# Moving the output weights' mean row to GpSimd, and moving sums, turns, squares and products in a Fourier and SoLU kernel

## The chip, the cores and the metric

The kernel runs on one core of one Trainium2 chip. The metric is the device time of one execution in microseconds. Five engines have queues of their own, each worked off in order: TensorE (PE in the profile, with its weight loads as PEld), VectorE (DVE), ScalarE (ACT), GpSimd (POOL) and SyncE (SP, which here only issues DMAs). POOL issues DMAs too. They wait for each other through semaphores.

## What is computed

The input x has 8 sequences of 3136 tokens with 256 features. Its two-dimensional Fourier transform over tokens and features is taken, and the real part goes through one expert:

```python
X = np.fft.fft(np.fft.fft(x, axis=1), axis=2).real     # (8, 3136, 256) -> (25088, 256)
h = X @ w_in                                            # 1024 hidden features
sm = softmax(h)
solu = h * sm
ln = (solu - solu.mean(-1)) / sqrt(solu.var(-1) + 1e-6) * g_ln
out = ln @ w_out                                        # (25088, 256)
```

All arithmetic is in 32-bit floats; the weights arrive as 64-bit floats and are narrowed on the chip.

## The kernel before, in words

**The transform.** 3136 is 49 x 64. The sequences go in four pairs (`pairs`). For each pair `load` fetches the rows and their mirror rows, `add_mirror` adds the two, `fold` or `fold_part` (L149, L150, L174) adds and subtracts the features k and 256 - k, `transform1` (L214) does the 49-point part on TensorE, `keep` writes the result to DRAM and `turn` (L230) reads it back with the other axis on the partitions. `transform2` (L242) does the 64-point part for one `k1`; `take2` (L248) copies its result to SBUF as `q`. The feature transform is multiplied into w_in once, at the start: `product_in` (L665) makes the even half of `Wi` (h = 0), its odd half (h = 1) and the row `w_mid` (h = 2, spread over all partitions), and `keep_in` (L669) copies each from PSUM.

**Units.** A unit is one `k1` of one pair: 128 rows, 25 units per pair, 100 in all. Except for k1 = 0 a unit has two signs: the hidden row is the even part plus or minus the odd part. `up` (L277) multiplies `q` with one half of `Wi` into a PSUM tile of two banks (`h0` or `h1`, one buffer each). `even` (L283) adds `r` times `w_mid` to the even part on DVE, where `r` is one row of `q` laid over the partitions, by a small DMA on SP (`spread`, L253) or, for units 2 and 3, by TensorE (`column`, L268 and L270). `join` (L291) makes h for a sign and its maximum, `expo` (L299) is exp on ACT, `product` (L306) multiplies h with it on DVE, `square` (L313) sums squares on ACT, `stats` (L326, L328) and `power` (L339, L368) make the scale per row. `join(s)` reads `ev`, or the sign 0 row, and the PSUM tile `h1`, so `up` of the next unit's odd half waits for it.

**Down.** The hidden rows are needed with the hidden features on the partitions. For units 0 to 3 `turn_whole` does that on TensorE: transposes (L394) of a sign go to two of the four banks `result(1..4)`, and copies bring them to `uT`, for sign 0 on ACT at once (L399), for sign 1 through the list `t.wait` on DVE (L868) or, in step 4, on ACT (L873). From unit 4 on `turn_both` (L377) transposes blocks of 32 x 32 on DVE, and `move_blocks` (L413) sends the blocks to their places, 16 DMAs on SP for two units. The product with w_out for a unit of two signs takes seven block products instead of eight (`Down`, L451): it needs four sums of parts of the rows (`sums`, L444, on POOL, the last three units' on DVE) and four sums of parts of the weights (`weight_sums`, L425, once, on POOL). `finish` scales and adds the blocks P5 (L508) and X (L510) on DVE and the rows are stored (L536 on POOL, the other half by SP). Units with one sign use `down` (L519). The layer norm's mean is taken out of w_out: `centre` sums the rows of `Wo` on TensorE (L698), scales the sum on ACT (L699), and subtracts it from `Wo` in one DVE instruction (L700).

**The order of the work** is written out by hand. Until the first pair's last first transform there is the weights' part: pieces of raw words are split into exponent and mantissa (`exponent`, `confine`, `narrow`; L571, L593 to L595, L607 to L615). Then comes the opening loop over steps 0 to 4 (`whole` = 4): step i turns unit i - 1, joins and finishes unit i, and begins unit i + 1 (`begin`: up, even, up, and the second transform of unit i + 3). Then the main loop: step i does up, even, join, expo, product, square and turn of unit i, the seven products of unit i - 5 (`lag`) and the sums of unit i - 4. The other pairs' mirror sums (POOL), folds (DVE), first transforms (PE) and loads are threaded into fixed steps; the folds of pair 1 run in steps 4 to 19. `behind(i, t)` makes an instruction wait for the last `product` of unit t; the helper gives as its reason "two operands at a time from SBUF".

Of the kernel before, what the change touches and what calls it, by code (L numbers as in the profile page):

```python
# [34 lines left out]
WHOLE = 4  # L35

# [7 lines left out]
def kernel(  # L44
# [187 lines left out]
    def transform2(pr, k1):  # L232

        i, k = divmod(k1, KG)
        g = pr.g[i]
        table = T[0][:, :, k, :] if i == 0 else T[1][:, :, k1 - KG, :]
        ps = result(0)[:, 0 : KD * P]
        for h in range(KD):  # L240
            o = ps[:, h * P : (h + 1) * P].rearrange("p (b k) -> p b k", b=2)
            nc.tensor.matmul(o, g[:, k, h * P : (h + 1) * P], table,  # L242
                             start=(h == 0), stop=True, skip_group_check=True)
        return ps
# [27 lines left out]
    def up(t, c):  # L272

        ps = ps_h.tile([P, FF], FP32, tag=f"h{c}", name=f"ps_h{c}")
        for half in range(2):
            fs = slice(half * HW, (half + 1) * HW)
            nc.tensor.matmul(ps[:, fs], t.q[:, c * P : (c + 1) * P], Wi[:, c, fs], start=True, stop=True)  # L277
        return ps

    def even(t, ps):  # L280

        t.ev = fpool.tile([P, FF], FP32, tag="ev", name="ev", bufs=1)
        nc.vector.scalar_tensor_tensor(out=t.ev, in0=w_mid, scalar=t.r, in1=ps,  # L283
                                       op0=ALU.mult, op1=ALU.add)
# [99 lines left out]
    def turn_whole(t):  # L384

        uT = t.batch.uT[:, t.w].rearrange("p c i (n s) -> p c (i n) s", s=2)
        n = KF // 2
        t.wait = []
        for s in t.signs:
            for half in range(2):  # L390
                ps = result(2 * s + half + 1).rearrange("p (c k) -> p c k", c=n)
                for c in range(n):
                    f = half * n + c
                    nc.tensor.matmul(ps[:, c, :], t.u[s][:, f * P : (f + 1) * P], ident, is_transpose=True,  # L394
                                     start=(c == 0), stop=(c == n - 1), skip_group_check=True)
                if s:
                    t.wait.append((uT[:, half * n : (half + 1) * n, :, s], ps))
                else:
                    nc.scalar.copy(uT[:, half * n : (half + 1) * n, :, s], ps)  # L399
# [21 lines left out]
    def weight_sums():  # L421

        B11, B12, B21, B22 = [Wo[:, k : k + KF // 2, f : f + P] for k in (0, KF // 2) for f in (0, P)]
        for j, (a, b) in enumerate(((B12, B11), (B22, Ws[:, 0]), (B22, B12), (B21, Ws[:, 1]))):
            nc.gpsimd.tensor_tensor(out=Ws[:, j], in0=a, in1=b, op=ALU.subtract)  # L425
# [27 lines left out]
    class Down:  # L453
# [52 lines left out]
        def finish(self):  # L506
            o = self.t.ot[0][:, P:]
            nc.vector.scalar_tensor_tensor(out=o, in0=self.P5, scalar=self.rs[0], in1=o, op0=ALU.mult, op1=ALU.add)  # L508
            o = self.t.ot[1].rearrange("p (i d) -> p i d", i=2)
            nc.vector.scalar_tensor_tensor(out=o, in0=self.X.unsqueeze(1).to_broadcast([P, 2, P]),  # L510
                                           scalar=self.rs[1], in1=o, op0=ALU.mult, op1=ALU.add)
# [71 lines left out]
    def confine(unit, here=False):  # L583

        if unit is None:
            return
        if here:
            bits(unit, unit, -896.0, ALU.add, 0.0, ALU.max)
            bits(unit, unit, 255.0, ALU.min, 2.0 ** 23, ALU.mult)
            return  # L590

        u = unit.bitcast(FP32)
        nc.scalar.activation(out=u, in_=unit, func=ACT.Relu, bias=limits[:, 0:1])  # L593
        nc.scalar.activation(out=u, in_=u, func=ACT.Relu, bias=limits[:, 1:2], scale=-1.0)
        nc.scalar.activation(out=unit, in_=u, func=ACT.Identity, bias=limits[:, 2:3], scale=-(2.0 ** 23))  # L595
# [22 lines left out]
    class Weights:  # L618
# [40 lines left out]
        def product_in(self, h):  # L659
            ps = ps_h.tile([P, FF], FP32, tag=f"h{h % 2}", name="wps")  # L660
            for half in range(2):
                fs = slice(half * HW, (half + 1) * HW)
                for c in range(KD):
                    lhsT = self.m[:, c, :] if h == KD else self.Q[:, c, h * P : (h + 1) * P]
                    nc.tensor.matmul(ps[:, fs], lhsT, self.w_in[c][:, fs], start=(c == 0), stop=(c == KD - 1))  # L665
            return ps
# [27 lines left out]
        def centre(self):  # L694

            cs = result(0)[:, 0:D]
            for c in range(KF):
                nc.tensor.matmul(cs, ones, Wo[:, c, :], start=(c == 0), stop=(c == KF - 1))  # L698
            nc.scalar.mul(out=wbar, in_=cs, mul=1.0 / FF)  # L699
            nc.vector.tensor_tensor(out=Wo, in0=Wo, in1=wbar.unsqueeze(1).to_broadcast([P, KF, D]), op=ALU.subtract)  # L700
# [41 lines left out]
    with tc.manual_schedule():  # L742
# [30 lines left out]
        for c in range(NC):  # L773
# [10 lines left out]
            if c == NC - 1:  # L784
                for i in range(3):
                    weights.exponent_out(i)
            if c + 6 < NC:
# [8 lines left out]
            for s in range(CH // 2):  # L796
                transform1(first, c * CH // 2 + s)
            if c == 3:
                weights.keep_in(0, weights.product_in(0))

        turn(first, 0, nc.sync, 0, 2)
        turn(first, 0, nc.gpsimd, 2, KG)

        middle = weights.product_in(KD)
        confine(weights.units[0], True)
        for i in range(1, 3):
            confine(weights.units[i])
        weights.keep_in(KD, middle)
        weights.narrow_out(0)
        weights.exponent_out(3)  # L810
        confine(weights.units[-1])
        odd = weights.product_in(1)
# [4 lines left out]
        for t in units[:2]:  # L817
            take2(t, transform2(pairs[0], t.k1))
            spread(t)
            if t is units[0]:  # L820
                weights.keep_in(1, odd)
# [6 lines left out]
        def second_transform(i):  # L828
            if i < len(units):
                t = units[i]  # L830
                take2(t, transform2(pairs[t.p], t.k1))
                if i not in (2, 3):
# [26 lines left out]
        for i in range(whole + 1):  # L859
            cur = units[i]  # L860
            prv = units[i - 1] if i else None
            if prv:
                turn_whole(prv)
            for s in cur.signs:
                join(cur, s)
            if prv and i < whole:
# [4 lines left out]
            if prv and i == whole:  # L871
                for o, ps in prv.wait:
                    nc.scalar.copy(o, ps)  # L873
            if i == 0:
                begin(1)
            if i == whole:
# [5 lines left out]
            if i == 1:  # L882
                weights.centre()
                weight_sums()
            if i < whole:

                if i:
                    begin(i + 1)
                if 1 in cur.signs:
                    square(cur, 1)  # L890
                stats(cur)
                power(cur)
            else:
                for s in cur.signs:
                    square(cur, s)
                other_pairs(i, ahead, "mirror", cur)
                turn_both(cur)
# [4 lines left out]
            for work in ("mirror", "fold", "load") if i < whole else ("load",):  # L902
                other_pairs(i, ahead, work)
# [5 lines left out]


        fresh = True
        for i in range(whole + 1, len(units) + lag + 1):
# [18 lines left out]
            if i == len(units):  # L931
                for s in prv.signs:
                    square(prv, s)
            if prv:
# [14 lines left out]
            elif old:  # L949
                for s, ps in plain:  # L950
                    scale(old, s, ps)
            if cur:
# [6 lines left out]
            if seven:  # L959
                new.p3()  # L960
                new.p7()
                new.finish()
            if cur:
                other_pairs(i, ahead, "mirror")
            if by_seven(i + 1 - lag):
# [8 lines left out]
            if cur:  # L974
# [8 lines left out]
                turn_both(cur)  # L983
# [92 lines left out]
```

## Time and profile before

| what | us |
|---|---|
| median of 3 runs (lowest, highest) | 1135.96 (1133.18, 1139.01) |
| the profiled execution, its own time | 1132.91 |
| its span | 1130.9 |
| PE busy | 1092.3 (97%) |
| DVE busy | 987.4 (87%) |
| ACT busy | 800.5 (71%) |
| POOL busy | 796.3 (70%) |

The profile tells of one execution. The chain of work that ended last follows the program back from its end, at each step to what released it; the groups give each line's instructions, their count, busy time and mean; the waits say who idled for whom; the timeline lists instructions by start and duration; the windows give each engine's busy time in a stretch. A start is counted from the start of the span. POOL's own durations are rough; the spacing of its instructions tells more.

### The profile page before, as it was taken

Reading aid. Unit: us, or ns where it says so; the run is one execution under the profiler, and the core shown is the slowest. Engines: PE = TensorE matmul, PEld = TensorE weight load, DVE = VectorE, ACT = ScalarE, POOL = GpSimd, SP = SyncE. Lnnn points to the kernel's source line nnn. Section 1 sums busy time; section 2 is a strip of 40 time slices with the busy share of each in tenths; the row PEclk is TensorE's granted clock in tenths of the full one; section 3 lists DMA queues with packets and bytes.
Section 4 is the critical chain, followed back from the end, with each engine's and each line's share of the span. In section 5 each row is a group of like instructions: output and inputs, shape, how many; then the busy total and the mean of one; then the engine's idle time right before and its main releaser. Section 6 shows DMA issues by size and latency. Waiting matters only on the chain.

```text
span 1130.9 us, 21944 instructions
## 1 busy us (share of the span) xinstructions
PE 1092.3 (97%) x7030; PEld 872.2 (77%) x7030; DVE 987.4 (87%) x1442; ACT 800.5 (71%) x1945; POOL 796.3 (70%) x698
## 2 busy tenths in 40 slices
PE   2898999999999999999999999999999999999998
PEld 1556787887887787878877787878877788778888
DVE  7889989898889998898988998898888899898983
ACT  4667777777767777777767777777776777777761
POOL 3036888875795988865878788876686576766673
PEclk9999999999999999999999999999999999999999
DMA  9672798766998879876969798876788685965665
GB/s 246 207 196 57 169 189 205 174 150 147 165 207 159 188 174 186 192 152 144 169 149 186 170 191 187 197 178 148 152 160 156 132 164 116 161 142 112 140 135 119
DMA packets 459601, 185.77 MB, mean 164 GB/s; under 512 B 426870, under 2 KB 441470, under 8 KB 459488
## 3 DMA queue, kind: packets, MB, share of 16 engines
q1 hardware_dynamic: 445728, 146.22, 63.0%
q0 software_dynamic: 13760, 38.16, 13.1%
q8 instruction: 57, 0.93, 0.3%
q14 instruction: 56, 0.46, 0.1%
HBM read 44.78 MB, written 38.80 MB: 74 GB/s over the span
## 4 chain that ended last, share of the span: by engine, by line
PE 90%; DVE 4%; issue 2%; ACT 2%; DMA 2%; SPq 0%; POOL 0%; POOLq 0%; DVEq 0%; ACTq 0%
PE ps_m L451 52%; PE ps_h L277 28%; PE ps_m L214 5%; PE ps_m L242 4%; DMA raw_in<-in_moe_w_in_dram 1%; DVE h L291 1%; DVE u L306 1%; PE ps_m L519 1%; ACT h L313 1%; DVE ev L283 0%; DVE y L150 0%; PE wps L665 0%; DVE Wo L615 0%; DVE y L149 0%; ACT u L299 0%
## 5 line engine op out<-in xcount | busy, mean ns | idle before, releaser
L277 PE MATMUL ps_h<-Wi,q 128*128 128x512 f32 x800 | 362.4, 594 | 5.9 <-DVE nmax L291 5.1
L444 POOL TENSOR_TENSOR S<-uT 128x512 f32<-128x512 f32 x186 | 238.0, 1279 | 108.3 <-DVE u L306 34.5
L451 PE MATMUL ps_m<-Ws,S 128*128 128x128 f32 x2304 | 296.4, 275 | 0.0
L451 PEld LDWEIGHTS ps_m<-Ws,S 128*128 128x128 f32 x2304 | 279.8, 192 | 3.6 <-issue 0.4
L313 ACT ACTIVATE h<-u,usum 128x1024 f32<-128x1024 f32 x196 | 225.3, 1150 | 79.5 <-DVE u L306 79.0
L277 PEld LDWEIGHTS ps_h<-Wi,q 128*128 128x128 f32 x800 | 143.8, 190 | 152.0 <-issue 139.4
L306 DVE SCALAR_TENSOR_TENSOR u<-h,u 128x1024 f32<-128x1024 f32 x196 | 234.7, 1234 | 9.4 <-ACT u L299 9.4
L299 ACT ACTIVATE u<-h,nmax 128x1024 f32<-128x1024 f32 x196 | 223.8, 1143 | 6.0 <-DVE nmax L291 4.7
L377 DVE STREAM_TRANSPOSE v<-u 128x2048 f32<-128x2048 f32 x88 | 203.4, 2311 | 3.1
L451 PE MATMUL ps_m<-Wo,uT 128*128 128x128 f32 x1536 | 203.7, 276 | 0.0
L451 PEld LDWEIGHTS ps_m<-Wo,uT 128*128 128x128 f32 x1536 | 187.9, 192 | 1.0 <-issue 1.0
L291 DVE CUSTOM_DVE_ANT_0 h<-ev,ps_h 128x1024 f32<-128x1024 f32 x100 | 122.2, 1222 | 17.0 <-DVE ev L283 8.8
L536 POOL DMA_INDIRECT out_dram<-ot,idx x96 | 109.7, 1143 | 37.4 <-issue 12.5
L291 DVE CUSTOM_DVE_ANT_0 h<-h,ps_h 128x1024 f32<-128x1024 f32 x96 | 117.2, 1221 | 14.2 <-DVE nmax L291 0.5
L283 DVE SCALAR_TENSOR_TENSOR ev<-w_mid,r,ps_h 128x1024 f32<-128x1024 f32 x100 | 124.1, 1241 | 0.8 <-PE ps_h L277 0.7
L444 POOL TENSOR_TENSOR S<-uT,S 128x512 f32<-128x512 f32 x93 | 118.8, 1278 | 7.3
L444 POOL TENSOR_TENSOR S<-S,uT 128x512 f32<-128x512 f32 x93 | 118.7, 1277 | 7.3
L451 PE MATMUL ps_m<-Wo,S 128*128 128x128 f32 x768 | 101.5, 275 | 0.8 <-ACT ot L486 0.8
L451 PE MATMUL ps_m<-Ws,uT 128*128 128x128 f32 x768 | 101.8, 276 | 0.0
L242 PEld LDWEIGHTS ps_m<-T,g 128*128 128x128 f32 x400 | 60.1, 191 | 50.1 <-issue 45.7
L451 PEld LDWEIGHTS ps_m<-Wo,S 128*128 128x128 f32 x768 | 93.4, 192 | 1.0 <-issue 1.0
L214 PE MATMUL ps_m<-y,F 98*100 98x258 f32 (+3 forms) x288 | 70.4, 377 | 24.4 <-DVE y L162 22.1
(103 smaller groups left out, 1177.7 us busy)
## 6 DMA issues: line engine op xcount, KB each, us to landing
uT<-v SPq DMA_DIRECT2D x752, 128.0 KB
g<-zd POOLq DMA_DIRECT2D x72, 160.0 KB, 5.2
out_dram<-ot SPq DMA_DIRECT2D x176, 64.0 KB
xa<-in_x_dram SPq DMA_DIRECT2D x28, 392.0 KB
zd<-z SPq DMA_DIRECT2D x24, 400.0 KB
raw_in<-in_moe_w_in_dram SPq DMA_DIRECT2D x4, 512.0 KB
raw_out<-in_moe_w_out_dram SPq DMA_DIRECT2D x2, 1024.0 KB
room<-in_x_dram SPq DMA_DIRECT2D x4, 392.0 KB
```

The costliest lines, as they stand in the source:

```text
L214: nc.tensor.matmul(o[..., cs], F[:, 2 * t + h, :], i[..., cs], start=first, stop=True, skip_group_check=True)
L242: nc.tensor.matmul(o, g[:, k, h * P : (h + 1) * P], table, start=(h == 0), stop=True, skip_group_check=True)
L277: nc.tensor.matmul(ps[:, fs], t.q[:, c * P : (c + 1) * P], Wi[:, c, fs], start=True, stop=True)
L283: nc.vector.scalar_tensor_tensor(out=t.ev, in0=w_mid, scalar=t.r, in1=ps, op0=ALU.mult, op1=ALU.add)
L291: nc.vector.tensor_tensor_reduce(out=t.h[s], in0=t.h[0] if s else t.ev, in1=t.odd, scale=1.0 if s else -0.5, scalar=3.0e38, op0=ALU.add, o ...
L299: nc.scalar.activation(out=t.u[s], in_=t.h[s], func=ACT.Exp, bias=t.nmax[:, s : s + 1], scale=-1.0, accum_out=t.esum[:, s : s + 1])
L306: t.last = nc.vector.scalar_tensor_tensor(out=t.u[s], in0=t.h[s], scalar=-1.0, in1=t.u[s], op0=ALU.mult, op1=ALU.mult, accum_out=t.usum[:, ...
L313: nc.scalar.activation(out=t.h[s], in_=t.u[s], func=ACT.Square, bias=t.usum[:, s : s + 1], scale=-float(FF), accum_out=t.ssq[:, s : s + 1])
L377: nc.vector.transpose(out=t.batch.v[:, :, t.w], in_=t.both.rearrange("p s (g n) -> p (s g) n", n=32))
L444: i = engine.tensor_tensor(out=S[j], in0=a, in1=b, op=op)
L451: nc.tensor.matmul(o, a[:, c], b[:, c], start=start and c == 0, stop=c == n - 1, skip_group_check=True)
L536: dma = nc.gpsimd.indirect_dma_start(out=out, out_offset=bass.IndirectOffsetOnAxis(ap=idx[:, i : i + 1], axis=0), in_=t.ot[s], in_offset=None)
```

## The change

1. Weights' part: in the last chunk `exponent_out` runs for two pieces instead of three, then the first piece is confined on DVE and narrowed at once; the remaining exponents follow later. The ACT instructions of the second piece's `confine` go between the last two first transforms. The odd half of w_in (`product_in(1)`) goes in three parts between and behind the first transforms instead of behind `w_mid`'s product, and is copied before `w_mid`, which is now copied after the first two units' `q`. The second transforms of units 0 and 1 use two banks.
2. Step 1: the copies of unit 0's turn, its `stats` and `power` go behind unit 1's `expo` on ACT. The mean row's product goes behind unit 2's beginning (`mean_out`, bank 4 of the banks), its scaling to the end of the step (`keep_mean`).
3. Step 2: the mean row is subtracted from `Wo` on POOL, in four instructions of 128x512, the first behind unit 2's products; the DVE instruction is gone.
4. Step 3: POOL makes the four sums of unit 1 here, before in step 5. Step 4: `weight_sums` here, behind unit 4's products, before in step 1.
5. Unit 5: `r` times `w_mid` is added on TensorE (two more matmuls with one row), and `even` is a copy on ACT.
6. Main loop: where the next step's unit i + 1 - 5 has one sign (i = 29, 54, 79) the DVE turn of unit i goes behind the next unit's `join`.
7. End: the last unit's `square` and `stats` go behind the scalings of the unit in hand; in the last step `p7` and its finish come before `p3` and its finish.

```diff
+MIDDLE = (5,)
...
     def up(t, c):
+        whole_even = c == 0 and t.p == 0 and t.k1 in MIDDLE
...
+        if whole_even:
+            for half in range(2):
+                fs = slice(half * HW, (half + 1) * HW)
+                nc.tensor.matmul(ps[:, fs], t.q[0:1, P : 2 * P], w_mid[0:1, fs], start=False, stop=True)
...
     def even(t, ps):
+        if t.p == 0 and t.k1 in MIDDLE:
+            nc.scalar.copy(t.ev, ps)
+            return
...
-    def turn_whole(t):
+    def turn_whole(t, late=False):
...
-                if s:
+                if s or late:
                     t.wait.append((uT[:, half * n : (half + 1) * n, :, s], ps))
...
-    def weight_sums():
+    def weight_sums(t):
...
+            if j == 0:
+                behind(i, t)
...
-        def centre(self):
-            cs = result(0)[:, 0:D]
+        def mean_out(self):
+            self.cs = result(3)[:, 0:D]
             for c in range(KF):
-                nc.tensor.matmul(cs, ones, Wo[:, c, :], start=(c == 0), stop=(c == KF - 1))
-            nc.scalar.mul(out=wbar, in_=cs, mul=1.0 / FF)
-            nc.vector.tensor_tensor(out=Wo, in0=Wo, in1=wbar.unsqueeze(1).to_broadcast([P, KF, D]), op=ALU.subtract)
+                nc.tensor.matmul(self.cs, ones, Wo[:, c, :], start=(c == 0), stop=(c == KF - 1))
+        def keep_mean(self):
+            nc.scalar.mul(out=wbar, in_=self.cs, mul=1.0 / FF)
+        def centre(self, t):
+            for c in range(0, KF, 2):
+                i = nc.gpsimd.tensor_tensor(out=Wo[:, c : c + 2], in0=Wo[:, c : c + 2],
+                                            in1=wbar.unsqueeze(1).to_broadcast([P, 2, D]), op=ALU.subtract)
+                if c == 0:
+                    behind(i, t)
...
+        weights.product_in(1, (2, 3), odd)
         middle = weights.product_in(KD)
-        confine(weights.units[0], True)
-        for i in range(1, 3):
-            confine(weights.units[i])
-        weights.keep_in(KD, middle)
-        weights.narrow_out(0)
-        weights.exponent_out(3)
-        confine(weights.units[-1])
-        odd = weights.product_in(1)
+        confine(weights.units[0], parts=(2,))
+        for i in range(2, 4):
+            weights.exponent_out(i)
+        confine(weights.units[1])
+        weights.keep_in(1, odd)
+        confine(weights.units[2])
         for i in range(1, 4):
             weights.narrow_out(i)
...
-            if prv and i == whole:
+            if i in (1, whole):
                 for o, ps in prv.wait:
                     nc.scalar.copy(o, ps)
...
+            if i == 1:
+                stats(prv)
+                power(prv)
...
-            if i == 1:
-                weights.centre()
-                weight_sums()
+            if i == 2:
+                weights.centre(cur)
...
+                if i == 1:
+                    weights.mean_out()
...
                 other_pairs(i, ahead, "mirror", cur)
+                weight_sums(cur)
                 turn_both(cur)
...
+            if i == whole - 1:
+                sums(units[1], cur)
...
+        def plain_next(i):
+            return i + 1 < len(units) and whole < i and not by_seven(i + 1 - lag)
...
             if cur:
                 for s in cur.signs:
                     join(cur, s)
-            if seven:
+            if prv and plain_next(i - 1):
+                turn_both(prv)
+            if seven and old is units[-1]:
+                new.p7()
+                new.finish(1)
                 new.p3()
+                new.finish(0)
+            elif seven:
+                new.p3()
+                new.finish(0)
                 new.p7()
-                new.finish()
+                new.finish(1)
...
-            if by_seven(i + 1 - lag):
+            if by_seven(i + 1 - lag) and i > lag:
                 sums(units[i + 1 - lag], prv, nc.vector if i > len(units) else nc.gpsimd)
...
-                turn_both(cur)
+                if not plain_next(i):
+                    turn_both(cur)
```

## The prediction

> **What bounds the kernel now.** I read the chain of waits first, for the engine that sets the end; then the windows, for the stretch in which it does not; then the timeline, for what releases whom there.
>
> ```profile
> PE 90%; DVE 4%; issue 2%; ACT 2%; DMA 2%; SPq 0%; POOL 0%; POOLq 0%; DVEq 0%; ACTq 0%
> ```
>
> TensorE holds nine tenths of the chain. The next lines are the windows of the opening: stretch, its length, busy time of PE, PEld, DVE, ACT and POOL with counts, granted clock, DMA share, GB/s.
>
> ```profile
> 80.00:100.00 20.00, 17.11 (x77) 10.73 (x76) 18.99 (x30) 17.56 (x40) 6.00 (x6) 1.00 0.08 18
> 100.00:120.00 20.00, 18.66 (x111) 14.15 (x112) 19.30 (x28) 14.71 (x38) 17.50 (x17) 1.00 0.61 133
> 120.00:140.00 20.00, 20.00 (x126) 15.81 (x126) 18.04 (x31) 14.79 (x37) 17.77 (x17) 1.00 0.74 170
> ```
>
> From 80 to 100 DVE is full (18.99 of 20) and PE is not; from 120 PE is. The timeline has PE without a gap from about 109.7 until 1083, so time is to be won or lost in three places only: before the hand-over at 109.7, at the few gaps in between, and behind 1083. Inside the gapless part, PE's instructions count, and the change adds none there. Clock: 1.00 in these lines, so durations carry over.
>
> Next, timeline lines: start, duration, engine, line, operation, and in brackets the idle time before it and who ended it.
>
> ```profile
> 65.80 3.62 PE L698 MATMUL ps_m<-Wo,ones 128*128 128x256 f32 x16
> 71.16 0.36 ACT L699 ACTIVATE wbar<-ps_m 128x256 f32<-128x256 f32 x1
> 71.55 2.29 DVE L700 TENSOR_TENSOR Wo<-Wo,wbar 128x2048 f32<-128x2048 f32 x1 [0.43 <-ACT wbar L699]
> ...
> 92.11 1.27 POOL L142 TENSOR_TENSOR xa<-xa,xb 98x510 f32<-98x510 f32 x1
> 94.16 1.22 DVE L306 SCALAR_TENSOR_TENSOR u<-h,u 128x1024 f32<-128x1024 f32 x1
> 96.61 2.51 POOL L142 TENSOR_TENSOR xa<-xa,xb 98x510 f32<-98x510 f32 x2 [3.23 <-DVE u L306]
> 102.73 0.86 DVE L149 TENSOR_TENSOR y<-xa 98x254 f32<-98x254 f32 x1
> 103.28 1.22 POOL L444 TENSOR_TENSOR S<-uT 128x512 f32<-128x512 f32 x1
> 103.52 1.25 DVE L150 TENSOR_TENSOR y<-xa 98x254 f32<-98x254 f32 x1
> ...
> 606.77 1.27 POOL L444 TENSOR_TENSOR S<-uT 128x512 f32<-128x512 f32 x1
> 607.03 2.10 DVE L306 SCALAR_TENSOR_TENSOR u<-h,u 128x1024 f32<-128x1024 f32 x1
> 608.00 1.71 POOL L339 TENSOR_TENSOR rs<-v,neg_half 128x2 f32<-128x2 f32 x1
> ```
>
> Two things are to be seen. The subtraction holds DVE for 0.43 + 2.29 = 2.72 us. And POOL was idle while DVE made unit 4's products (93.39 to 96.61): there L306 took 1.22. At 607, beside a sum on POOL, it took 2.10, and POOL's small operation behind took 1.71 instead of 0.69 at 91.46. Beside a sum, L149 and L150 took 0.86 and 1.25; at 93.4, beside none, 0.42 each.
>
> **The change part by part** (times on the clock of before).
>
> *Weights' part: 0.* DVE no longer waits 1.12 us at 46.7 for the raw output weights, so it would be ready for unit 0's `ev` at 57.8 instead of 58.98. But `w_mid`'s copy is now last on ACT, to about 56.35, behind unit 0's and 1's `q`, and the first `up` needs the PSUM tile that it empties: it begins at 56.4 instead of 55.79. The second `ups` come at 60.3 as before (60.31). Bounds -0.5 and +0.5; I take 0.
>
> *Steps 1 and 2, mean row: -0.4.* DVE sheds 2.72 us. ACT does `expo` of unit 1 before unit 0's copies, from 66.1 instead of 67.46, and unit 1's products end at 69.84 instead of 71.1. So far 1.3 us ahead. But PE's 3.62 us of L698 lay beside DVE work at 65.8; now it stands on PE between the second transform of unit 4 and `turn_whole` of unit 1. That turn begins at 69.65 + 0.31 + 1.82 + 0.44 + 3.35 (start to start of the 16) = 75.57 instead of 73.64; ACT's copies of it, queued ahead of `expo` of unit 2, start at 76.2 (before 75.97), `expo` at 77.35 (76.97). DVE, ahead until here, waits there. Unit 2's products end at 81.0 instead of 81.46. Of 2.72 us about 0.4 remain.
>
> *Subtraction on POOL: 0.* Four instructions of 128x512 at 1.28 (mean of the L444 groups) are 5.1 us, from 81.1 to 86.3, behind unit 2's products. DVE meanwhile does `ev`, joins and copies out of PSUM, which ran undisturbed beside `weight_sums` in 73.9 to 79 (ev 1.28, join 1.22). Unit 3's products begin at 86.35; a broadcast operand is in no POOL row, and bounds of once and twice 1.28 each give 0 to 0.9 of collision. I take once.
>
> *Unit 1's sums in step 3: +3.4.* POOL's queue then has unit 3's small operation (to 91.7), a mirror sum (to 93.0) and the four sums, 93.0 to 98 or later. DVE does two folds from 93.0 and unit 4's two products from 93.8, all with two operands in SBUF, where before POOL stood still. By the rows, each of these four takes 0.4 to 0.9 longer beside a sum, and the two engines alternate, so that the sums are stretched over all four DVE instructions. Ends of L149 and L150 in 102.7 to 104.8 are 1.17 apart, 0.83 over the undisturbed 0.34 spacing; L306 loses 0.88. Four times about 0.9 is some 3.7: products end at 99.8 instead of 96.05, that is +3.4 against before's 96.45. Bounds: 0 (POOL late enough to miss) and four whole sums, 5.1.
>
> [...] If each of the four waited for a whole sum, the part would cost 5.1 rather than 3.4.
>
> *Unit 5's `even` on ACT: 0 under this delay.* DVE sheds 1.24 (98.80), ACT gets a copy of about 1.0 behind unit 4's squares and `stats`; those follow the products by 2.2 (96.45 to 98.66), so the copy ends at 103.0 and the join starts at 103.05 instead of 100.21. The two more matmuls, 4 x 0.43 = 1.7 us on PE, end before DVE comes: PE has slack up to 93.25 and 95.74. Without the delay the join would start at 99.35.
>
> *`weight_sums` in step 4:* they take the place of unit 1's sums in step 5. The folds there collide with them as they did with the sums; a product gets some 0.4 more. They end at 106.3, and the first product that needs them is at 109.8. Unit 5's products end at 110.35 instead of 107.1, and PE is gapless from there. **Opening: +3.2.**
>
> *Late turns: -0.6.* At units 30, 55 and 80 PE waits for DVE, as in the first of these lines:
>
> ```profile
> 371.72 1.96 PE L277 MATMUL ps_h<-Wi,q 128*128 128x512 f32 x4 [0.88 <-DVE nmax L291]
> ...
> 1098.16 1.13 PE L451 MATMUL ps_m<-Wo,S 128*128 128x128 f32 x8 [0.83 <-ACT ot L486]
> ...
> 1120.24 0.69 DVE L444 TENSOR_TENSOR S<-uT 128x512 f32<-128x512 f32 x1 [0.63 <-DMA out_dram<-ot]
> 1125.81 0.48 DVE L510 SCALAR_TENSOR_TENSOR ot<-ps_m,rs,ot 128x256 f32<-128x256 f32 x1 [0.45 <-PE ps_m L451]
> 1127.06 0.96 POOL L536 DMA_INDIRECT out_dram<-ot,idx  x1 [5.29 <-DVE ot L510]
> ```
>
> The three waits are 0.88, 0.88 and 0.26, and a turn of 2.3 us leaves the way of each. Next, though, PE waits for a `q` copy behind the squares on ACT (376.24), which lets 0.26, 0.33 and 0.26 through. The turn that is late also starts 16 DMAs on SP some 4 us later (368 to 372); everything queued behind them on SP follows, and one sum with it, priced at 0.3. Bounds -2.0 and +0.9.
>
> *Tail: -0.9.* With the squares behind the scalings the wait of 0.83 goes, but what is late next is the last batch's DMAs: SP is busy from 1081.46 to 1116.55 and a sum at 1120.24 waits for them. I cost it at 0. With `p7` first, L510 comes at 1124.92 instead of 1125.81 and POOL's store, the last, 0.89 earlier. Bounds -0.9 and 0.
>
> **Sum:** +3.2 - 0.6 - 0.9 = +1.7 on 1132.91 is 1134.6. The profiled execution lies 3.05 under the median of 1135.96; the same +1.7 there gives **1137.7**.
>
> **Rivals.** *No collision:* the sums miss the products, or hold DVE less than the rows say. Then the opening gives -0.4 from step 2 and -0.3 from `ev`, in all -0.7 - 0.6 - 0.9 = -2.2: 1133.8. For it: everything is within a microsecond of missing. Against: POOL is idle from 86.3 and has nothing to hold it back. *Everything DVE sheds counts:* L698 hides after all, no collision; 2.72 + 1.24 = 3.96 in the opening, -5.5 in all: 1130.5. For it: DVE is 18.99 of 20 full. Against: the PE order of step 1. *POOL stays late (slower):* after `weight_sums` POOL must catch up with the sums of unit 2 and on. Before, its sums of step 7 ended at 124.42 and the folds began at 125.04, a margin of 0.62. If POOL is late by more than this, the folds of every step to 19 lose 1.2, of which 0.85 is slack (waits of 0.39 and 0.46 per step); 0.35 x 14 = 5 more, +6.7 in all: 1142.7.
>
> **How the numbers follow.** Forecast 0.48, with its own range 1135 to 1140 (the bounds of the sums, 0 to 5.1, lead outside it only together with a rival); no collision 0.21; all counts 0.17; POOL late 0.14. The range of 1130.5 to 1142.0 leaves out about half of "all counts" and half of the slow case, with some of the forecast's tails 2 in 10. A difference of 0.5%, 5.7 us, is about the least that a measurement of this kernel can tell from none: faster means below 1130.3, where two thirds of "all counts" lie (0.11) and a little of "no collision" (0.01), 0.12; slower means above 1141.6, 0.14; the rest 0.74.
>
> **What would show it.** `turn_whole` of unit 1 on PE at about 75.6, DVE idle before unit 2's products; L306 of unit 4 at around 2 us and its folds near 1, with sums on POOL between them; PE gapless from about 113, not 109.7; no DVE wait at units 30, 55, 80; last L510 before the last L508, and the last store 0.9 earlier behind it. Wrong if unit 4's products take 1.22 each (then 1133.8 or less), or if POOL's sums still run beside the folds in steps 8 to 19 (then over 1140).

## The result, and the profile after

The changed kernel takes 1142.35 us (median of 22 runs, 1136.22 to 1146.04) where the kernel before takes 1135.95 (22 runs of its own): a ratio of 1.0052, 95% interval 1.0041 to 1.0063, or some 5.9 us slower (the ratio is not that of the medians, which differ by 6.4). Its profiled execution took 1143.01 with a span of 1141.2. The chain of waits on its page breaks off at the last store, so windows, waits and timelines stand in its place.

The windows of the changed kernel's opening (stretch, length, busy PE, PEld, DVE, ACT, POOL with counts, granted clock, DMA share, GB/s):

```profile
60.00:80.00 20.00, 16.87 (x57) 9.71 (x56) 14.13 (x21) 10.44 (x22) 0.73 (x2) 0.91 0.93 252
80.00:100.00 20.00, 19.70 (x90) 11.92 (x89) 16.19 (x26) 17.20 (x36) 9.39 (x9) 1.00 0.02 5
100.00:120.00 20.00, 15.99 (x74) 11.25 (x73) 19.34 (x21) 12.78 (x30) 18.27 (x17) 0.91 0.24 60
120.00:140.00 20.00, 20.00 (x129) 15.99 (x129) 19.03 (x31) 15.04 (x39) 16.77 (x14) 1.00 0.77 161
```

Two stretches stand out: DVE is idle for 5.9 of 20 us from 60 to 80 (3.2 before), and PE for 4.0 from 100 to 120 (1.3 before; pair 0's last fold ends 3.1 us later in this trace, so the windows do not lie over quite the same work). In both the granted clock is 0.91 where before it was 1.00. The timeline shows the second stretch (the lines of code have moved: L150, L151 and L175 are the fold, L315 the product, L455 a sum):

```profile
97.46 1.27 POOL L143 TENSOR_TENSOR xa<-xa,xb 98x510 f32<-98x510 f32 x1
98.70 1.49 POOL L455 TENSOR_TENSOR S<-uT 128x512 f32<-128x512 f32 x1
98.77 1.71 DVE L150 TENSOR_TENSOR y<-xa 98x254 f32<-98x254 f32 x1 [0.30 <-POOL xa L143]
100.27 1.36 POOL L455 TENSOR_TENSOR S<-S,uT 128x512 f32<-128x512 f32 x1
100.40 1.50 DVE L151 TENSOR_TENSOR y<-xa 98x254 f32<-98x254 f32 x1
101.71 1.35 POOL L455 TENSOR_TENSOR S<-uT,S 128x512 f32<-128x512 f32 x1
101.83 1.25 DVE L175 TENSOR_TENSOR y<-xa,xb 98x2 f32<-98x2 f32 x1
103.00 1.21 DVE L315 SCALAR_TENSOR_TENSOR u<-h,u 128x1024 f32<-128x1024 f32 x1
103.02 2.09 POOL L455 TENSOR_TENSOR S<-uT 128x512 f32<-128x512 f32 x1
104.15 2.05 DVE L315 SCALAR_TENSOR_TENSOR u<-h,u 128x1024 f32<-128x1024 f32 x1
...
109.13 5.31 PE L279 MATMUL ps_h<-Wi,q 128*128 128x512 f32 x8 [3.67 <-ACT ev L290]
```

DVE and POOL take turns in these rows. The fold's instructions, 0.42, 0.42 and 0.16 before, take 1.71, 1.50 and 1.25, and the second product 2.05. Even the fold of 98x2 elements lasts until the sum beside it (101.71 to 103.06) is done. PE then stands 3.67 us in front of unit 5's join, where before it stood 0.18 and 0.88 for unit 5's two `up`.

How far this goes is best counted within each trace, from the end of pair 0's last fold, since the loads ahead of it scatter: that end lies between 44.92 and 50.95 in fourteen traces, and between 44.92 and 50.03 in the nine whose code up to there is that of before. M is the time from there to the first join of unit 7, by when PE has no gaps left. All from the DVE rows of the timelines:

| kernel | unit 1's products end | unit 2's products end | unit 4, first join to end of products | M | ratio (interval) |
|---|---|---|---|---|---|
| before | 26.19 | 36.56 | 6.01 | 76.59 | 1 |
| changed | 25.73 | 38.83 | 10.34 | 82.99 | 1.0052 (1.0041, 1.0063) |
| a_sums | 25.34 | 36.76 | 6.01 | 83.55 | 1.0073 (1.0049, 1.0096) |
| a_step1 | 26.82 | 36.31 | 10.33 | 80.47 | 1.0049 (1.0032, 1.0067) |
| a_weights | 25.62 | 37.05 | 10.32 | 81.21 | 1.0060 (1.0041, 1.0079) |
| a_fill | 26.05 | 39.16 | 10.32 | 83.35 | 1.0056 (1.0038, 1.0075) |
| b_ends | 25.77 | 36.11 | 6.01 | 76.14 | 1.0004 (0.9986, 1.0021) |
| b_sums | 25.42 | 35.75 | 10.31 | 80.57 | 1.0036 (1.0022, 1.0051) |
| b_pool | 25.42 | 36.78 | 6.01 | 76.80 | 1.0002 (0.9987, 1.0017) |
| best2 | 25.99 | 35.49 | 6.67 | 78.15 | 1.0016 (0.9997, 1.0034) |
| best6 | 25.44 | 33.91 | 6.00 | 75.22 | 0.9986 (0.9972, 1.0000) |
| best7 | 25.43 | 33.89 | 6.00 | 75.39 | 0.9988 (0.9976, 1.0000) |
| best8 | 25.41 | 33.87 | 6.00 | 74.63 | 0.9990 (0.9975, 1.0006) |
| best9 | 25.41 | 33.88 | 6.01 | 73.89 | 0.9977 (0.9962, 0.9992) |

The start of a trace still scatters behind the loads: before, b_ends and b_sums have the same code as far as unit 2's products, and these end at 36.56, 36.11 and 35.75. Nearly all of that lies ahead of unit 1's products; from these it is 10.37, 10.34 and 10.33. So a difference under 0.8 us in the second column or in M tells nothing by itself, and where the order of step 1 is that of before the distance from unit 1's products is the better count.

M is 6.40 longer after the change; of that 2.27 is there by the end of unit 2's products, 4.33 come in unit 4, 0.78 are won by unit 5's `even` (from the products' end to the next join 2.91 instead of 3.69), and 0.6 lost again in step 5, whose folds now meet `weight_sums`.

Behind the opening, PE's waits in the changed kernel (who waits for whom, us in all, times, longest):

```profile
PE ps_m L215 <- ACT q L249: 2.0, 2, 1.0
PE ps_m L462 <- DMA out_dram<-ot: 1.2, 1, 1.2
PE ps_m L462 <- issue: 1.0, 1, 1.0
PE ps_m L462 <- ACT ps_m L488: 0.8, 1, 0.8
```

The three waits for `nmax` at the plain steps (2.0 in all) are gone. In their place the next step's first transform or product waits for a copy on ACT, 1.00, 1.01 and 0.80. (The line with "issue" is one step at 366 in which a fold meets the sums; best8 below, whose main loop is that of before, has such a wait of 2.45 at 359, put down to POOL, so it is not the change's.)

### The profile page after: what moved, and what is told of

It reads as the page before. It is cut to its first block, busy times and chain, and to the rows that moved or that the text cites. A ratio compares the mean times of both kernels' runs of the same rounds, so it can differ in the third digit from the quotient of the medians.

```text
span 1141.2 us, 21944 instructions
## 1 busy us (share of the span) xinstructions
PE 1095.8 (96%) x7034; PEld 875.1 (77%) x7034; DVE 990.6 (87%) x1440; ACT 799.6 (70%) x1946; POOL 804.2 (70%) x702
## 5 line engine op out<-in xcount | busy, mean ns | idle before, releaser
L455 POOL TENSOR_TENSOR S<-uT 128x512 f32<-128x512 f32 x186 | 239.4, 1287 | 107.7 <-DVE u L315 34.7
L315 DVE SCALAR_TENSOR_TENSOR u<-h,u 128x1024 f32<-128x1024 f32 x196 | 236.3, 1241 | 8.7 <-ACT u L308 8.6
L455 POOL TENSOR_TENSOR S<-uT,S 128x512 f32<-128x512 f32 x93 | 118.9, 1278 | 7.3
L455 POOL TENSOR_TENSOR S<-S,uT 128x512 f32<-128x512 f32 x93 | 118.7, 1277 | 7.3
L462 PEld LDWEIGHTS ps_m<-Ws,uT 128*128 128x128 f32 x768 | 93.9, 192 | 0.0
```

The source lines that it names most:

```text
L315: t.last = nc.vector.scalar_tensor_tensor(out=t.u[s], in0=t.h[s], scalar=-1.0, in1=t.u[s], op0=ALU.mult, op1=ALU.mult, accum_out=t.usum[:, ...
L455: i = engine.tensor_tensor(out=S[j], in0=a, in1=b, op=op)
L462: nc.tensor.matmul(o, a[:, c], b[:, c], start=start and c == 0, stop=c == n - 1, skip_group_check=True)
```

## The experiments

My theory after the result: unit 1's sums in step 3 hold DVE (the collision). Rivals: step 1's new order; the granted clock; the weights' part; the loads at the start. Of the first four kernels (a_) three undo one part of the changed kernel and one keeps PE busy; the next three (b_) add to the kernel before one part of the change or, b_ends, two.

### a_sums: the sums back in step 5

```diff
-            if i == whole - 1:
-                sums(units[1], cur)
...
-            if by_seven(i + 1 - lag) and i > lag:
+            if by_seven(i + 1 - lag):
```

> The changed kernel with unit 1's sums back in step 5. I count the opening from the end of the last fold of pair 0 (44.92 before, 48.01 after the change) to the first transform of step 5 (108.72, 118.22): 63.8 before, 70.2 after. Collision theory: from the first join of unit 4 to the end of its products it takes 5.9 again instead of 10.3, TensorE's wait of 3.67 in front of unit 5's join shrinks below 1, the opening is 4 to 6 us shorter and the time near 1137; the folds of step 5 then meet weight_sums and sums and lose about 1 more than before. Rival (the loss lies in steps 1 and 2, on TensorE and ScalarE): the products of unit 4 end earlier but the join of unit 5 does not, and the time stays within 1.5 us of 1142.

1145.19 us where I expected 1137: no gain. Unit 4 is undisturbed (6.01), as expected; the gain is lost one step later, where I had allowed 1 us. POOL now has `weight_sums` and the sums in one row, from 101.77 to 115.40, and step 5's fold meets both:

```profile
106.01 1.14 DVE L150 TENSOR_TENSOR y<-xa 98x254 f32<-98x254 f32 x1
107.07 2.95 DVE L151 TENSOR_TENSOR y<-xa 98x254 f32<-98x254 f32 x1
109.94 1.25 DVE L175 TENSOR_TENSOR y<-xa,xb 98x2 f32<-98x2 f32 x1
...
112.26 2.30 DVE L315 SCALAR_TENSOR_TENSOR u<-h,u 128x1024 f32<-128x1024 f32 x1
```

PE waits 4.52 us in front of step 5's first transform. So the sums' place alone is not the root: the change also has `weight_sums` 30 us later (from 29.0 us behind the last fold to 59.5), in a stretch that is full already, and in these two kernels whichever of POOL's two rows comes there collides.

### a_step1: step 1 as before, subtraction on POOL

```diff
-                turn_whole(prv, i == 1)
+                turn_whole(prv)
...
+            if i == 1:
+                weights.mean_out()
+                weights.keep_mean()
             if i == 2:
                 weights.centre(cur)
```

> The changed kernel with step 1 as before (unit 0's copies, its stats and power at once, the mean row's product ahead of unit 2's beginning), the subtraction still on POOL. Theory of steps 1 and 2: TensorE's wait of 1.96 for the late copies is gone and the granted clock stays at 1.00 between 70 and 85; from the last fold to the end of unit 2's products it takes 35 to 36.5 us instead of 38.75 (before 36.54), and the time falls by 2 to 3.5 us to about 1139 to 1140. Collision theory alone: this shifts everything earlier but the sums still meet unit 4's folds and products (10.3 from join to end of products), so no more than those 2 to 3.5 us come back. If DVE's shed 2.72 us count in full, 34 us to the end of unit 2's products.

PE's wait and the first dip of the clock are gone, and unit 2's products end at 36.31: M is 2.5 shorter. The time, 1141.73, is above the 1139 to 1140 that I expected and cannot show it clearly (the intervals overlap). The collision stays, 10.33. From unit 1's products to unit 2's it takes 9.49, against 10.37 before: DVE's 2.72 us bring only 0.9. In the trace ACT's queue holds the rest back:

```profile
78.69 0.37 ACT L249 COPY q<-ps_m 128x256 f32<-128x256 f32 x1 [2.34 <-PE ps_m L243]
78.96 1.15 ACT L322 ACTIVATE h<-u,usum 128x1024 f32<-128x1024 f32 x1
```

ACT stands 2.34 us for the `q` copy with unit 1's second square, ready since 75.95, behind it; copies and `expo` of unit 2 follow.

### a_weights: the weights' part as before

```diff
-        weights.product_in(1, (2, 3), odd)
         middle = weights.product_in(KD)
-        confine(weights.units[0], parts=(2,))
+        confine(weights.units[0], True)
...
+        weights.keep_in(KD, middle)
+        weights.narrow_out(0)
...
+        odd = weights.product_in(1)
```

> The changed kernel with the weights' part as before. Theory that the new order costs because w_mid is copied last: from the last fold to unit 0's even sum it takes 14.1 us (as before) instead of 14.9, and the time falls by 0.8 us, to 1141.5. Rival, that the weights' part is neutral and unit 0's even sum waited only for its small DMA: no difference beyond 0.5 us in that stretch. Neither expects more than 1 us in the time, so the stretch in the trace decides.

Unit 0's even sum starts 14.76 after the last fold, 14.87 in the changed kernel; the time, 1143.07, is no better. Over all traces it is 12.83 to 14.76 with the old part (nine, mean 13.35) and 13.40 to 15.19 with the new one (five, mean 14.34), where DVE waits for the small DMA of `r` (2.07 in the changed kernel). So the part may cost up to 1 us, and this run does not settle it.

### a_fill: PE kept busy in its second wait

```diff
                 elif old:
+                    if old is units[0]:
+                        down(old, 0, result(1)[:, 0:D])
```

> The changed kernel in which TensorE multiplies unit 0's hidden rows with w_out twice over in step 5 (16 more matmuls, 3.5 us, with the same result), in the stretch in which it otherwise waits 3.67 us for unit 5's even copy. Clock theory: the granted clock stays at 1.00 from 108 to 113 where it was 0.50 for 3.4 us, unit 5's second and unit 6's first up take 3.6 instead of 5.31, and the time falls by up to 1.7 us although TensorE does more. Rival (clock has no part, or the path is DVE's): no change, or later by what the 3.5 us overrun.

The clock is 1.00 from 104 to 116 (mean of 6 runs 0.9993, of the changed kernel's 22 runs 0.9968), each up takes 1.98 again, and the time does not move (1142.89). Unit 5's and 6's joins come at 61.41 and 72.65 from the last fold (61.10 and 72.31): DVE's folds set the pace there, and the half clock costs nothing that shows in this kernel (1142.89 without it, 1142.35 with it). The rival holds for this dip; in b_sums, below, it does not.

### b_ends and b_sums: parts 6 and 7 alone, the sums in step 3 alone

b_ends is the kernel before with these edits of the change, and with the last unit's `square` and `stats` moved as in part 7:

```diff
+            if prv and plain_next(i - 1):
+                turn_both(prv)
+            if seven and old is units[-1]:
+                new.p7()
+                new.finish(1)
...
-                turn_both(cur)
+                if not plain_next(i):
+                    turn_both(cur)
```

> The kernel before with parts 6 and 7 alone (late turns, squares, order of p7 and p3); its opening is that of before, so its trace also tells how far the loads at the start differ from run to run: by the theory that the end of pair 0's last fold (44.92 before, 48 to 49.4 in five kernels with the changed opening) is chance and not the change, it may lie anywhere from 44.9 to 49.4 here. Theory that late turns and tail are worth what the changed kernel's trace shows: the wait in front of the late pair's second up goes, one of 1.0 in front of the next first transform comes, and the end is 0.5 to 1.5 us earlier; time 1134.5 to 1136. Rival, late turns cost: 1137 or more.

1136.71 us, ratio 1.0004: late turns and end together are worth nothing that shows, a result between the 1134.5 to 1136 of my theory and the rival's 1137 or more. The last fold ends at 50.03 here, with the loads' code of before, so the late start of the changed kernel's trace is chance.

```diff
+            if i == whole - 1:
+                sums(units[1], cur)
...
-            if by_seven(i + 1 - lag):
+            if by_seven(i + 1 - lag) and i > lag:
```

> The kernel before with unit 1's sums in step 3 as the only edit. Collision theory: from the first join of unit 4 to the end of its products it takes 9.5 to 10.4 instead of 5.9, the fold's two large instructions 1.2 or more each instead of 0.42; step 5's folds, with no sums beside them, take 0.42 each again (1.2 back), and from the last fold to step 5's first transform it takes 66 to 67.5 instead of 63.8; time 1138.5 to 1140. Rival (the sums only meet DVE there because the changed kernel is late): 5.9 stays, time 1135 to 1137.

The rival falls. The kernel before with this one edit loses 0.36% (4.1 us; 1141.8, above the 1138.5 to 1140 that I expected), its clock also dips at unit 5 (0.83 from 100 to 120), and step 4 shows the changed kernel's rows to within 0.01:

```profile
96.22 1.71 DVE L149 TENSOR_TENSOR y<-xa 98x254 f32<-98x254 f32 x1 [0.29 <-POOL xa L142]
97.85 1.50 DVE L150 TENSOR_TENSOR y<-xa 98x254 f32<-98x254 f32 x1
99.27 1.26 DVE L174 TENSOR_TENSOR y<-xa,xb 98x2 f32<-98x2 f32 x1
...
101.59 2.05 DVE L306 SCALAR_TENSOR_TENSOR u<-h,u 128x1024 f32<-128x1024 f32 x1
...
107.21 6.72 PE L277 MATMUL ps_h<-Wi,q 128*128 128x512 f32 x8 [4.53 <-DVE ev L283]
...
121.09 0.35 DVE L508 SCALAR_TENSOR_TENSOR ot<-ps_m,rs,ot 128x128 f32<-128x128 f32 x1 [1.85 <-PE ps_m L451]
```

The last two rows show that here the collision costs time through PE too. PE waits 4.53 us for unit 5's even sum, the eight matmuls behind it take 6.72 us where 3.70 is the time at 1.00 (60.31 in before), and PE has no gap from there on. At the 0.50 of the changed kernel's dip, the 0.83 of the window makes 6.8 us at half clock. In step 6 DVE waits 1.85 us for PE, where it waited 0.26 before. Unit 6's first join is 2.2 us later than before (68.11 from the last fold against 65.90), unit 7's 4.0. So some 1.8 us of the loss (4.0 less 2.2) came with the half clock, by my estimate from one trace; no run kept PE busy in this wait.

### b_pool: the subtraction alone on POOL, in its old place

```diff
-            nc.vector.tensor_tensor(out=Wo, in0=Wo, in1=wbar.unsqueeze(1).to_broadcast([P, KF, D]), op=ALU.subtract)
+            for c in range(0, KF, 2):
+                nc.gpsimd.tensor_tensor(out=Wo[:, c : c + 2], in0=Wo[:, c : c + 2],
+                                        in1=wbar.unsqueeze(1).to_broadcast([P, 2, D]), op=ALU.subtract)
```

> The kernel before with the subtraction on GpSimd in four instructions at its old place in step 1, weight_sums behind it, as the only edit. If what DVE sheds counts in full, unit 2's products end 33.8 us after the last fold instead of 36.56, and the time falls by 2.7 to 1133.3. My theory is that TensorE and ScalarE then set the pace (the q copy behind unit 4's second transform, squares and copies ahead of unit 2's expo) and weight_sums, 5 us later than before, meet unit 2's products (1.7 to 2.1 instead of 1.23 each): 36 to 37.5 us, and the time within 1 us of before.

As my theory had it: 36.78, M +0.2, ratio 1.0002. From unit 1's products to unit 2's it takes 11.36, 1.0 more than before: the shed time is more than lost again. The four instructions, with their broadcast operand, take 4.98 together, 1.25 each (1.28 is the mean of the sums in before), and unit 2's products take 2.01 and 2.28 beside `weight_sums`, where they took 1.24 and 1.25 before.

### best2, best6 to best9: where POOL's work fits

best2 is the changed kernel with the edits of a_step1 and a_sums and this one:

```diff
             if i == 2:
                 weights.centre(cur)
+                weight_sums(cur)
...
-                weight_sums(cur)
                 turn_both(cur)
```

> The changed kernel with step 1 as before, unit 1's sums back in step 5, and weight_sums in step 2 directly behind the subtraction. Collision theory: unit 4's folds and products run undisturbed (5.9 to 6.2 from join to end), weight_sums meet unit 3's products instead (1 to 1.8 us more there), and with unit 5's even sum on ScalarE the opening takes 62.5 to 64.5 (70.2 after the change), so that the time is 1134 to 1137. Rival, that POOL's later work pushes its sums into the folds of all steps to 19: the opening as said, but the stretch from step 5's first transform to the end 3 to 6 us longer than 1022, time 1139 to 1142.

1138.78 us, above the 1134 to 1137 that I expected. Unit 3's products lie beside `weight_sums`, and that step takes 2 us longer (35.49 to 45.17, before 36.56 to 44.21). Better than the changed kernel, no better than before.

best6 is the kernel before with the subtraction on POOL and two moves, which answer to b_pool's rows and to ACT's in a_step1; best7 adds the changed kernel's parts 5 to 7.

```diff
                 weights.centre()
-                weight_sums()
+                square(cur, 1)
+            if i == 2:
+                weight_sums(cur)
...
-                if 1 in cur.signs:
+                if 1 in cur.signs and i > 1:
                     square(cur, 1)
```

> The kernel before with the subtraction on GpSimd in step 1, weight_sums behind unit 2's products (the 5.3 us in which DVE has no instruction with two operands in SBUF), and ScalarE's second square of unit 1 ahead of unit 2's beginning, so that it does not stand behind the q copy that waits for TensorE. Theory (collisions and ScalarE's order ate what DVE shed): unit 2's products take 1.23 each and end 33.5 to 35 us after the last fold (before 36.56, b_pool 36.78), the opening is 61 to 62.5 (before 63.8), and the time falls by 1.3 to 2.8 us, to about 1134. Rival (TensorE sets the pace of steps 2 and 3 whatever DVE does): 36 or more, opening 63.3 to 64, no change.

> As best6, with the changed kernel's unit 5 (even sum on TensorE and ScalarE), late turns and end. Theory: without collisions unit 5's even copy on ScalarE is worth 0.5 to 0.9 in front of unit 5's join (from the end of unit 4's products to that join 3.69 before, 3.65 in best2), the opening 60.3 to 62, the end 0 to 0.9 earlier, the time 1132.5 to 1134.5. Rival: ScalarE's squares and stats of unit 4 stand in front of the copy, the join comes no earlier, and the time is that of best6.

In best6 unit 2's products end at 33.91, 2.65 earlier; 0.75 of this is there already at unit 1's products, where the code is that of before, and 1.9 come behind them (8.47 against 10.37): now most of the shed time counts. An estimate of the square's share: b_pool without what its two slow products lost (2.01 + 2.28 against 2 x 1.22, some 1.85) would stand at 9.5, where a_step1 does, so the square's move is worth about 1.0. Of the 1.9, 1.3 go again in step 3, where the join waits 0.93 for ACT's square, which stands behind the next `q` copy as it did in step 1. M is 1.37 shorter (0.6 from unit 1's products), the ratio 0.9986. best7 gains 0.5 in front of unit 5 and loses it in step 5's folds; the two kernels measure alike.

best8 is best6 with the square's move in step 2 too, best9 is best8 with `p7` ahead of `p3` in the last step (b_ends' third to fifth added line):

```diff
+                if i in (1, 2):
+                    square(cur, 1)
                 if i:
                     begin(i + 1)
...
-                if 1 in cur.signs:
+                if 1 in cur.signs and i > 2:
                     square(cur, 1)
```

> As best6, with the second square ahead of the next beginning in step 2 too, since there DVE waited 0.93 and 0.42 us for ScalarE. Theory (ScalarE's order held back what the free DVE could do): unit 3's products end 41.3 to 41.9 us after the last fold (before 44.21, best6 42.86), the opening is 60.8 to 61.6 (63.8, 62.44), and the time is 2 to 3 us under that of before. Rival: weight_sums now run into unit 3's products, or TensorE's up holds the join, and the opening stays at 62 to 62.5.

> As best8, with p7 and its finish ahead of p3's in the last step, the one edit of the changed kernel's end that I priced at 0.9. Theory: from the last p1 to the last store's start 0.8 to 0.9 less than before (1118.99 to 1127.06, 8.07, and 6.6 in the changed kernel), and the time 0.5 to 1 us under that of best8, which only the trace can show. Rival: SyncE's store of the other half lands last, and the end is the same.

M is 1.96 and 2.70 shorter than before, 1.2 and 1.9 from unit 1's products (the code of the opening is the same in both; in best8's trace unit 3's products waited 0.62 for `expo`). In best9 the subtraction and `weight_sums` fill exactly stretches in which DVE's work has at most one full-width operand in SBUF, and in which it takes what it takes in before with POOL idle (even sums 1.28, joins 1.22, two copies 1.28):

```profile
72.46 4.99 POOL L705 TENSOR_TENSOR Wo<-Wo,wbar 128x512 f32<-128x512 f32 x4 [0.79 <-ACT wbar L703]
80.59 1.28 POOL L425 TENSOR_TENSOR Ws<-Wo 128x512 f32<-128x512 f32 x1 [2.45 <-DVE r L270]
...
84.42 1.29 POOL L425 TENSOR_TENSOR Ws<-Wo,Ws 128x512 f32<-128x512 f32 x1
```

Unit 2's products end at 80.44, unit 3's begin at 85.73, and `weight_sums` lie between. From the last `p1` to the last store's start it takes 6.81 in best9 and 7.93 in best8, which lacks the move. best9 takes 1133.53 us, ratio 0.9977 (0.9962 to 0.9992): faster than the kernel before by an interval that just leaves out 1 (one kernel of thirteen that were measured), and clearly faster than the changed one. best8's time (1135.9, 0.9990) is not told apart from that of before.

## Why the prediction was right or wrong

**The direction and the collision were right, the size was not, and the clock was left out.** The forecast was +1.7, the measurement is +5.9 (4.7 to 7.2). That lies outside the forecast's own 1135 to 1140. The wide range, up to 1142.0, just holds it (1.0052 x 1135.96 = 1141.9), and by luck: it reached so far for a part of "POOL late", which did not happen. The time is close to the slow rival's 1142.7, but not by its mechanism: from unit 7's first join to the end the trace takes 1010.2 (1141.2 - 48.01 - 82.99), and 1009.4 before, so no 5 us are lost to POOL's lateness in the later steps, and from step 8 on the large folds of pair 1 take 0.41 to 0.42 in both traces.

- *Bound, and where time can be won:* right. From 120 to 140 PE is busy throughout again, and M accounts for the result: +6.4 in the opening (+4.6 in a_weights, which had no dip of the clock in step 1), +0.8 at the late turns, -1.1 in the end: 4.3 to 6.1 in all. (The traces' own stretch behind M differs by +0.8 rather than -0.3; the wait of 1.03 at 366 is in it.)
- *Weights' part, 0:* open between 0 and 1 us late; the bound of 0.5 may have been too narrow.
- *Steps 1 and 2, -0.4:* failed. The sum has PE begin `column` at 69.65, behind the late copies without naming the wait, and turn unit 1 5.92 us later, with durations carried over at a clock of 1.00. `column` came at 70.45 on the clock of before, after a wait of 1.96, and the clock did not stay:

```profile
73.54 0.38 PE L269 MATMUL ps_m<-ones,q 1*128 1x1 f32 x2 [1.96 <-ACT uT L906]
73.85 2.83 PE L279 MATMUL ps_h<-Wi,q 128*128 128x512 f32 x4
76.47 1.06 PE L243 MATMUL ps_m<-T,g 128*128 128x128 f32 x4
77.33 4.08 PE L716 MATMUL ps_m<-Wo,ones 128*128 128x256 f32 x16
```

Behind the wait the clock is at half (0.50) from 74.9 to 78.3, and the up, the second transform and the mean row's product take 2.83, 1.06 and 4.08, where they took 1.98, 0.61 and 3.62 before. Four kernels have this order. With the dip (changed, a_fill) the turn of unit 1 begins 7.71 and 7.72 behind `column`, and unit 2's products end at 38.83 and 39.16; without (a_sums, a_weights) it is 6.03 and 6.02, and 36.76 and 37.05. So of some 2.1 us between the pairs 1.7 lie in PE's slower instructions; the other 0.4 are there when `column` begins. Counted from unit 0's even sum, which takes the scatter at the start out, unit 2's products end after 22.3 to 22.8 without the dip and 24.0 with it, 22.5 to 22.9 in before, b_ends and b_sums: the term was about 0 without and 1.1 to 1.5 with it. The changed kernel's 22 runs point the same way (1140.1 on average in the five with a mean clock of 0.998 or more, 1142.3 in the eight with 0.997, 1142.7 in the nine with 0.996 or less); no run took the dip alone away here.
- *Subtraction, 0 on POOL itself:* right, once 1.25 per instruction, and unit 3's products undisturbed at 1.21 and 1.22.
- *Sums in step 3, +3.4:* right in kind and place, mis-sized: the stretch from unit 4's first join to the end of its products grows by 4.3 in five kernels, alike to 0.03. I counted four collisions of 0.9; the two large folds lost 1.29 and 1.08, the first product nothing, the second 0.83, and the fold of 98x2, which I left out, 1.09. Four whole sums, my upper bound, are 5.1; the measured 4.3 lies between 3.4 and that.
- *Unit 5's `even`:* right. The join came 2.91 behind the products; I had said 3.25.
- *Late turns, -0.6:* wrong sign. I had the `q` copies behind the squares leave a gain of 0.26, 0.33 and 0.26 of the three waits. PE now waits 1.00, 1.01 and 0.80 for copies on ACT, so that 2.8 stand against 2.0 before: +0.8.
- *Tail, -0.9:* right for the squares (0: PE's 0.83 turned into a wait for the last DMAs, 0.94 to 2.22 in the eight kernels with part 7), and for `p7` somewhat too small: 6.6 from the last `p1` to the last store against 7.9 to 8.1 without the move, 1.3, of which some 1.1 are left at the end of the span.
- The rival "everything DVE sheds counts" falls with a_step1 and b_pool, where ACT's order and `weight_sums` take it; with both mended, in best6, 1.9 of the 2.72 count.

## What to carry to other kernels

In these traces work moved from DVE to POOL cost DVE nothing beside instructions with at most one full-width operand in SBUF (best9: even sums 1.28 and joins 1.22, as with POOL idle), and cost it beside those with two (b_pool: products of 2.01 and 2.28 instead of 1.24 and 1.25). Lay POOL's instructions against DVE's row by row, the smallest instructions and all that the moved work delays included, before counting a gain. When a full engine is relieved, read next what stands ready behind a waiting instruction in the other engines' queues: here, with one square behind one copy, 2.7 us counted as 0.9 (a_step1), and with the square ahead of it as 1.9 (best6). Count from a point in the trace that the change cannot have moved, and look how far traces of the same code differ there. Look at the clock behind a wait that PE is given: behind the 4.53 us in b_sums, with no gap of PE after it, the half clock cost some 1.8 us more by my estimate, and behind the 3.67 us in the changed kernel nothing that a_fill shows.

## What the runs showed of the hardware

A wait of PE of 1.96 us in step 1 was followed by a half clock in two of four kernels with the same code there: the changed one (0.50 from 75 to 78, 3.4 us in all) and a_fill, but not a_sums and a_weights (1.00 from 72 to 80, behind waits of 1.95 and 1.96). A wait of 2.45 in best8 (at 359) was followed by none: the products behind it take 1.06 to 1.11 for eight matmuls, as ahead of it. The five waits of 3.65 to 4.53 in steps 4 and 5 were each followed by slower matmuls. In the changed kernel the clock was 0.50 from 109 to 112, 3.4 us in all; for the others the length is my estimate from the clock of the 20 us windows, with 0.50 for the dip: 3.4 to 3.8 us in a_step1 (0.91), some 6.8 in a_weights and b_sums (0.83) and in a_sums (0.85 and 0.98). What sets these lengths, and which wait is followed by a dip, is not shown.

The fold of 98x2 elements, a DVE instruction of 0.16 us in step 4 of before, took 1.25 beside POOL's sum in the changed kernel and 1.26 in b_sums. It lost 1.09 there, the folds of 98x254 elements beside it 1.29 and 1.08: in these rows the loss did not go with the instruction's own size.
